# Attention into a tanh-shrink MLP: q and k fetched by squares of 32 and turned on VectorE from the fourth batch on, and the last store cut in two

## The chip, the cores and the metric

The kernel runs on one core of a Trainium2 chip. The metric is the time of one execution in microseconds, taken on the device. Its engines appear in the profile as PE (TensorE, with PEld for its weight loads), DVE (VectorE), ACT (ScalarE), POOL (GpSimd) and SP (SyncE, which here only issues transfers). Each takes its instructions in the order in which the program has them, and they wait for each other by semaphores.

## What is computed

Two blocks in a row. Attention: batch 8, 12 heads, 448 tokens, head width 64, with q and k normed by row before the product. Then an MLP of 3584 tokens, width 768, hidden width 2048:

```
rmsnorm(x, g) = x / sqrt(mean(x * x, axis=-1) + 1e-06) * g
scores = (1 / sqrt(64)) * rmsnorm(q, g_q) @ rmsnorm(k, g_k).T
attn   = exp(scores - max(scores)); attn = attn / (sum(attn) + 1e-09)
x      = (attn @ v), heads side by side: 3584 x 768
h = x @ w_in;  g = h - tanh(h);  out = g @ w_out
```

All data are float32 (the weights arrive as float64 and are rounded in the kernel).

## The kernel before

Work is cut into 48 **steps** (`steps`, L162): eight batches of six head pairs. A step s runs through several stages, and the stages of neighbouring steps are interleaved in a **slot**. There are three kinds: `first_slot` (L787) for the first batch, in which the weights are rounded; `early_slot` (L821) for the second; and `slot` (L849) for all others. The order inside a slot is written out by hand. In slot s the kernel finishes step s (sums of the exponentials, values, division), makes the scores of step s+1, turns q and k of step s+2, squares and norms those of step s+3 and loads those of step s+4. v of step s+2 is loaded here too.

Between these pieces `run(ns)` (L766) takes matmuls of the MLP from a generator, as many as fill the given time at 2.4 elements per ns. `gap_ns` (L778) spreads a batch's MLP evenly over its six slots: from the third batch on a `gap` is 14 matmuls, four gaps make a slot, and a matmul is two records in the trace. Whoever comes after a `run` in the program comes after its matmuls, and the instructions that empty their banks, in every engine's queue.

**q and k before.** `fetch` (L93) loads q with four neighbouring tokens on a partition (`"h (p c) d -> p h (c d)"`, 112 partitions, one transfer), k with three neighbouring keys on each of 128 partitions and 64 rest keys (four transfers). `squares_of` (L117) squares both on ScalarE. `norm_of` (L123) sums the squares on VectorE (L129), scales (L130), and takes the power -1/2 on GpSimd (L131), once for q and once for k. q is scaled by VectorE (`norm_q`, L400); k is not, its factor being the `scale` operand of the exponential (L444). `turn` (L406) makes both head-width-major: four TensorE transposes of k into one PSUM bank (L411), copied out by ScalarE with `g_col`, the product of g_q, g_k and 1/8 (L413), and four of q (L415), copied out at L419. `qT` and `kT` have two buffers each.

**Scores.** `scores` (L425) multiplies kT by qT (L438) for three chunks of 128 keys and a last one of 64, and ScalarE takes the exponential (L443). `add` and `add_last` (L451, L462) sum the chunks on VectorE (L459, L460, L467), so that `totals` (L495) needs fewer matmuls. There are five PSUM banks for attention (`sc`) and three for the MLP (`mm`), each set taken in turn (`bank_of`, L194).

**The MLP.** Both layers use Strassen-Winograd: seven products of half size per group in the order 1, 5, 6, 2, 3, 7, 4 (`ORDER`, L168; `products`, L557; the matmuls are L578). Products 2, 3 and 7 go on in the banks of 1, 5 and 6, and product 4 takes a new bank; hence the next use of a bank waits until VectorE or ScalarE has read the last. In the first layer (`hidden`, L599) VectorE makes the sums (L634 to L648), ScalarE the tanh (L614), VectorE or GpSimd the difference (L615), and both make factors of the second layer (L625 to L627, L659). Work that is not urgent is put on a list (`late["todo"]`) and issued at the end of the next product. Weights come from scratch memory into a ring of six slots (`ring_load`, L375): at the start of a product the load of the fifth product from there is issued (L382, L384), in SP's queue, together with all other loads and stores.

**The output.** `project` (L681) makes the second layer. `store` (L667) turns a 128 x 448 result on VectorE by blocks of 32 (L673), putting tokens back in natural order by reading them with a stride, since in q's loading a partition holds four neighbouring tokens, and issues four transfers from SP (L676), each of 32 x 14 runs of 128 bytes. The tanh buffer's two copies serve as its target.

Of the kernel before, what the change touches and what calls it, by code (L numbers as in the profile page):

```python
# [9 lines left out]
F32 = mybir.dt.float32  # L10
I32 = mybir.dt.int32
U32 = mybir.dt.uint32
AF = mybir.ActivationFunctionType
ALU = mybir.AluOpType
AX = mybir.AxisListType
# [5 lines left out]
NCH = 4  # L21
# [68 lines left out]
    nc.gpsimd.tensor_tensor(out=bits, in0=bits, in1=raw[:, :, 0], op=ALU.add)  # L90


def fetch(nc, name, t, pair):  # L93

    S = pair.shape[1]
    P = 128
    KF, KR = S // P, S % P
    if name == "q":
        nc.sync.dma_start(
            out=t.rearrange("p h c d -> p h (c d)"), in_=pair.rearrange("h (p c) d -> p h (c d)", c=NCH)  # L100
        )
        return
    full, rest = pair[:, : KF * P].rearrange("h (p c) d -> h p c d", c=KF), pair[:, KF * P :]
    if name == "v":
        last = t[:, :, KF]
        nc.sync.dma_start(
            out=t[:, :, :KF].rearrange("p h c d -> p h (c d)"), in_=full.rearrange("h p c d -> p h (c d)")
        )
    else:
        last = t[:, KF]  # L110
        for h in range(2):
            nc.sync.dma_start(out=t[:, :KF, h], in_=full[h])
    for r in range(2):
        nc.sync.dma_start(out=last[r * KR : (r + 1) * KR], in_=rest.rearrange("h p d -> p h d"))
# [19 lines left out]
def bounded_path(tc, ctx, q, k, v, moe_w_in, moe_w_out, out, g_col, ident, ones, half_ones, neg_half, early):  # L134
# [17 lines left out]
    nc = tc.nc  # L152
    B, H, S, D = q.shape
    DFF, DM = moe_w_out.shape
    P = 128
# [19 lines left out]
    def pool(name, **kw):  # L175
        return ctx.enter_context(tc.tile_pool(name=name, **kw))
# [27 lines left out]
    def load(s, names):  # L204
        b, hp = steps[s]
        for name in names:
            src = {"q": q, "k": k, "v": v}[name]
            if s == 0 and name != "v":
                t = early[name]
            else:  # L210
                shape = [CP, 2, NCH, D] if name == "q" else [P, NCH, 2, D] if name == "k" else [P, 2, NCH, D]
                t = nat.tile(shape, F32, name=f"{name}_nat", bufs=3 if name == "v" else 2)
                fetch(nc, name, t, src[b, 2 * hp : 2 * hp + 2])
            loaded[name, s] = t


# [189 lines left out]
    def turn(s, tk, tq):  # L406
# [12 lines left out]
        nc.scalar.copy(out=qT, in_=tq[:, :S])  # L419
        turned[s] = rr, kT, qT  # L420

    def sc_bank():
        return bank_of("sc")

    def scores(s, c):  # L425

        rr, kT, qT = turned[s]
        halves, keys, n = (1, P, S) if c < KF else (2, KR, HS)
        name, bufs = ("p", 2) if c < 2 else ("p_full", 1) if c < KF else ("p_last", 2)
        if c == 1:  # L430
            p = probs[s, 1] = probs[s, 0]
        else:
            p = probs[s, c] = pp.tile([P, 2, 2 if c < 2 else 1, n], F32, name=name, bufs=bufs)
        tiles = [sc_bank() for _ in range(2)]
        for i in range(halves):
            for h in range(2):
                r = slice(h * D, (h + 1) * D)
                nc.tensor.matmul(  # L438
                    tiles[h][i * keys : (i + 1) * keys, :n], lhsT=kT[r, c * P : c * P + keys],
                    rhs=qT[r, i * n : (i + 1) * n], start=True, stop=True,  # L440
                )
        for h in range(2):
            nc.scalar.activation(  # L443
                p[:, h, c if c < 2 else 0, :], tiles[h][:, :n], AF.Exp, scale=rr[:, 0, 2 * c + h : 2 * c + h + 1]  # L444
            )

    def full(s):
# [103 lines left out]
    def part(name):  # L551
        return tp.tile([P, 2, HS], F32, name=name)
# [111 lines left out]

        return products(b, 0, SETS, 2, HC, moving, done_with)

    def store(b, n, y):  # L667

        o = part("th").rearrange("p f s -> p (f s)")
        nc.vector.transpose(out=o, in_=y.rearrange("r (c p) -> r p c", c=NCH))  # L673
        for i in range(P // BL):
            d = n * P + i * BL
            nc.sync.dma_start(  # L676
                out=out[b * S : (b + 1) * S, d : d + BL].rearrange("(j t) d -> t j d", t=BL),
                in_=o[i * BL : (i + 1) * BL].rearrange("t (j d) -> t j d", d=BL),
            )

    def project(b):  # L681
        g, t = late["g"], late["t"]
        low, high = slice(0, HS), slice(HS, S)
        moving = {
            1: lambda f: g[:, f, low], 2: lambda f: g[:, f + HF, low], 3: lambda f: g[:, f + HF, high],
            4: lambda f: t[:, 2, f], 5: lambda f: t[:, 0, f], 6: lambda f: t[:, 1, f], 7: lambda f: g[:, f, high],
        }

        def done_with(j):
            y1, y2, s1 = (part(n).rearrange("p f s -> p (f s)") for n in ("s2", "s5", "s1"))  # L690

            def use(p, bank):
                v = bank[:, :HS]
                if p == 1:
                    nc.scalar.copy(out=s1[:, low], in_=v)
                elif p == 5:
                    nc.vector.tensor_tensor(out=y2[:, low], in0=v, in1=s1[:, low], op=ALU.add)
                elif p == 6:
                    nc.vector.tensor_tensor(out=y1[:, high], in0=v, in1=s1[:, low], op=ALU.add)
                elif p == 2:  # L700
                    nc.scalar.copy(out=y1[:, low], in_=v)
                elif p == 7:
                    nc.vector.tensor_tensor(out=y2[:, high], in0=v, in1=y2[:, low], op=ALU.add)
                    nc.vector.tensor_tensor(out=s1[:, low], in0=v, in1=s1[:, low], op=ALU.add)
                elif p == 3:
                    nc.vector.tensor_tensor(out=y1[:, high], in0=v, in1=y1[:, high], op=ALU.add)
                    late["todo"].append(lambda: store(b, j, y1))
                elif p == 4:
                    nc.vector.tensor_tensor(out=y2[:, low], in0=v, in1=s1[:, low], op=ALU.add)
                    late["todo"].append(lambda: store(b, HC + j, y2))  # L710

            return use

        return products(b, 1, HC, 1, HF, moving, done_with)

    def project_first(b):

        g = late["g"]
        for fn in late["todo"]:
            fn()  # L720
        late["todo"] = []
        took = 4 * S / ENGINE_NS
        for m in range(CD * CF):
            k, f = m // CF, m % CF
            n = (k + HC) % CD
            if f == 0:
                bank = mm_bank()
            if k < HC:
                weight(CF + HF + HF * (m + 1) // (HC * CF))
            elif m < HC * CF + 2:  # L730
                keep_w_out(PIECES - 2 + m - HC * CF)
            elif (m - HC * CF) % 4 == 0 and m - HC * CF <= 4 * HF:
                for fn in late["keep"]:
                    fn()
                late["keep"] = []
                combine_w_out((m - HC * CF) // 4 - 1)
            elif m == CD * CF - 12:
                ring_load(2)
                for fn in late["keep"]:
                    fn()  # L740
            elif m == CD * CF - 10:
                ring_load(4)
            nc.tensor.matmul(  # L743
                bank[:, :S], lhsT=w_out_row(f, n // HC)[:, n % HC * P : (n % HC + 1) * P], rhs=g[:, f, :],
                start=(f == 0), stop=(f == CF - 1),
            )
            if f == CF - 1:
                y = part("s2").rearrange("p f s -> p (f s)")
                nc.scalar.copy(out=y, in_=bank[:, :S])
                store(b, n, y)  # L750
            yield took
        wp_stack.close()
        late["tg"] = pool("tg", bufs=1)

    def mlp():
        late["todo"], late["keep"] = [], []
# [27 lines left out]
    def has(s):  # L784
        return 0 <= s < NS
# [63 lines left out]
    def slot(s):  # L849

        gap = gap_ns(s)
        if has(s + 1):
            scores(s + 1, KF)
        dn = sc_bank()
        av = [sc_bank() for _ in range(2)]
        last_values(s, av)
        totals(s, dn)
        divide(s, values(s, av))
        if has(s + 1):
            for c in range(KF):  # L860
                scores(s + 1, c)
        if has(s + 2):
            load(s + 2, "v")
        run(gap / 2)
        if has(s + 1):
            add(s + 1)
        run(gap / 2)
        if has(s + 2):
            turn(s + 2, sc_bank(), sc_bank())
        if has(s + 3):  # L870
            squares(s + 3)
        if has(s + 4):
            load(s + 4, "qk")
        for work, n, share in ((add_last, 1, 1), (norm, 3, 0.5), (norm_q, 3, 1)):
            run(gap * share)
            if has(s + n):
                work(s + n)
        run(gap / 2)

    load(0, "qk")  # L880
    load(1, "qk")
# [352 lines left out]
```

## Time and profile before

| | before |
|---|---|
| median of 11 runs | 1456.95 us (1455.11 to 1462.48) |
| the profiled execution | 1460.36 us |
| its span, first to last instruction | 1458.5 us |
| VectorE busy | 812.8 us (56%) |
| ScalarE busy | 453.0 us (31%) |
| GpSimd busy | 478.0 us (33%) |
| share of the 16 DMA engines, SP's queue | 59.5% |
| packets under 512 bytes | 164,725 of 267,894 |
| mean granted TensorE clock | 0.990 |

How to read the profile. A group's row gives line, engine, operation, what is written and read with shapes, the count, then busy time and mean ns of one, then the time for which the engine sat idle before it and what ended that. The **chain** is followed back from the last instruction, each time to what released it or to the instruction before it on its engine; what is not on it could be longer without moving the end. "issue" is time in which nothing shown was waited for. Durations are of one profiled execution; records of TensorE overlap, so the sum of their means is more than the time they take.

### The profile page before, as it was taken

How to read it: one execution, taken by the hardware profiler on the slowest of the kernel's cores; microseconds unless marked ns; L12 is line 12 of the kernel's file. 1: busy time of each engine (PE TensorE's matmuls, PEld its weight loads, DVE VectorE, ACT ScalarE, POOL GpSimd, SP SyncE). 2: the span in 40 equal slices, each digit the busy share in tenths (PEclk: the TensorE clock that was granted, in tenths of full speed). 3: DMA queues.
4: the chain of work that ended last, by engine and by line, in shares of the span. 5: the costliest groups of instructions: out<-in, count | busy, mean ns of one | idle time of the engine just before them, and what ended most of it. 6: DMA issues, size and time to landing. Idle time of an engine off the chain costs nothing.

```text
span 1458.5 us, 25920 instructions
## 1 busy us (share of the span) xinstructions
PE 1425.6 (98%) x10272; PEld 1202.1 (82%) x10272; DVE 812.8 (56%) x1246; ACT 453.0 (31%) x850; POOL 478.0 (33%) x378
## 2 busy tenths in 40 slices
PE   6999899999999999999999999999999999999997
PEld 3568654479988998899889989988998899899997
DVE  4999889766445564446644565446654456432312
ACT  6765553133212332223322233123322233211100
POOL 4656465223511243204421234212341134211310
PEclk9999899999999999999999999999999999999999
DMA  8769778854665555565536645654466555455663
GB/s 187 162 191 261 239 208 216 240 154 138 194 167 140 157 183 164 147 173 170 186 112 191 171 140 160 189 155 148 142 199 170 144 159 167 141 162 172 186 191 97
DMA packets 267894, 250.71 MB, mean 172 GB/s; under 512 B 164725, under 2 KB 210037, under 8 KB 267765
## 3 DMA queue, kind: packets, MB, share of 16 engines
q1 hardware_dynamic: 267760, 248.97, 59.5%
q8 instruction: 83, 1.36, 0.4%
q14 instruction: 47, 0.38, 0.1%
q10 hardware_dynamic: 4, 0.00, 0.0%
HBM read 215.48 MB, written 33.42 MB: 171 GB/s over the span
## 4 chain that ended last, share of the span: by engine, by line
PE 90%; DVE 5%; DMA 2%; SPq 2%; ACT 1%; issue 1%; POOL 0%; ACTq 0%
PE mm L578 64%; PE sc L438 9%; PE sc L489 6%; PE mm L743 4%; PE sc L477 1%; PE sc L510 1%; PE sc L411 1%; PE sc L415 1%; DVE w_out L82 1%; DVE rs L515 1%; DVE w_out L78 1%; DVE w_out L79 1%; DVE w_out L320 1%; DMA w_in<-w_out 0%; PE mm L489 0%
## 5 line engine op out<-in xcount | busy, mean ns | idle before, releaser
L131 POOL TENSOR_TENSOR rr<-rr,neg_half 112x8 f32<-112x8 f32 x96 | 156.5, 1649 | 370.6 <-DVE rr L130 370.5
L578 PE MATMUL mm<-xT,w_f 128*128 128x224 f32 x1392 | 276.6, 354 | 0.0
L578 PEld LDWEIGHTS mm<-xT,w_f 128*128 128x128 f32 x1392 | 261.3, 190 | 9.1 <-issue 9.1
L578 PE MATMUL mm<-gT,w_f 128*128 128x224 f32 x1344 | 263.0, 354 | 0.0
L578 PEld LDWEIGHTS mm<-gT,w_f 128*128 128x128 f32 x1344 | 252.8, 190 | 11.4 <-issue 11.1
L578 PE MATMUL mm<-tt,w_f 128*128 128x224 f32 x1044 | 209.6, 353 | 0.0
L615 POOL TENSOR_TENSOR gT<-s,th 128x448 f32<-128x448 f32 x96 | 117.9, 1236 | 260.9 <-ACT th L614 260.9
L578 PE MATMUL mm<-tg,w_f 128*128 128x224 f32 x1008 | 200.4, 353 | 0.0
L578 PEld LDWEIGHTS mm<-tt,w_f 128*128 128x128 f32 x1044 | 196.6, 190 | 3.9 <-issue 3.9
L578 PEld LDWEIGHTS mm<-tg,w_f 128*128 128x128 f32 x1008 | 189.5, 190 | 0.0
L438 PE MATMUL sc<-qT,kT 64*128 64x448 f32 (+1 forms) x960 | 169.9, 496 | 11.9 <-ACT p_last L443 8.9
L443 ACT ACTIVATE p<-sc,rr 128x448 f32<-128x448 f32 x192 | 106.0, 638 | 125.0 <-PE sc L438 125.0
L438 PEld LDWEIGHTS sc<-qT,kT 64*128 64x128 f32 (+1 forms) x960 | 73.4, 166 | 83.2 <-issue 48.8
L614 ACT ACTIVATE th<-s 128x448 f32<-128x448 f32 x96 | 55.5, 579 | 134.6 <-DVE s L640 56.6
L443 ACT ACTIVATE p_last<-sc,rr 128x224 f32<-128x224 f32 x96 | 37.8, 447 | 187.8 <-PE sc L438 187.7
L515 DVE RECIPROCAL rs<-sc 128x224 f32<-128x224 f32 x42 | 65.3, 1555 | 32.1 <-PE sc L510 32.0
L489 PE MATMUL sc<-p,v_nat 128*32 128x224 f32 x1344 | 79.1, 353 | 0.0
L538 POOL TENSOR_TENSOR tt<-xT,tt 128x224 f32<-128x224 f32 x23 | 17.1, 743 | 188.2 <-DVE xT L523 188.2
L743 PE MATMUL mm<-gT,w_out 128*128 128x448 f32 x192 | 76.9, 558 | 0.0
L523 DVE TENSOR_TENSOR xT<-sc,rs 64x224 f32<-64x224 f32 x168 | 65.2, 388 | 9.6 <-PE sc L489 2.2
L743 PEld LDWEIGHTS mm<-gT,w_out 128*128 128x128 f32 x192 | 36.9, 196 | 37.7 <-issue 36.7
L459 DVE TENSOR_TENSOR rows<-p 128x896 f32<-128x896 f32 x38 | 42.2, 1111 | 42.0 <-ACT p L443 42.0
(123 smaller groups left out, 1598.3 us busy)
## 6 DMA issues: line engine op xcount, KB each, us to landing
w_f<-w_in SPq DMA_DIRECT2D x196, 384.0 KB, 3.5
w_f<-w_out SPq DMA_DIRECT2D x147, 512.0 KB, 4.6
w_raw<-in_moe_w_out_dram SPq DMA_DIRECT2D x16, 768.0 KB, 5.1
out_dram<-th SPq DMA_DIRECT2D x192, 56.0 KB, 1.9
q_nat<-in_q_dram SPq DMA_DIRECT2D x47, 224.0 KB, 4.6
v_nat<-in_v_dram SPq DMA_DIRECT2D x48, 192.0 KB, 3.7
k_nat<-in_k_dram SPq DMA_DIRECT2D x94, 96.0 KB, 3.3
w_in<-w_out SPq DMA_DIRECT2D x21, 384.0 KB, 6.1
```

What stands on the lines that cost most here:

```text
L131: nc.gpsimd.tensor_tensor(out=r, in0=r, in1=neg_half[:rows], op=ALU.pow)
L438: nc.tensor.matmul(tiles[h][i * keys : (i + 1) * keys, :n], lhsT=kT[r, c * P : c * P + keys], rhs=qT[r, i * n : (i + 1) * n], start=True, ...
L443: nc.scalar.activation(p[:, h, c if c < 2 else 0, :], tiles[h][:, :n], AF.Exp, scale=rr[:, 0, 2 * c + h : 2 * c + h + 1])
L459: nc.vector.tensor_tensor(out=t, in0=p[0], in1=p[1], op=ALU.add)
L489: nc.tensor.matmul(av[n][r : r + BL, :HS], lhsT=v_nat[:, h, c, m * BL : (m + 1) * BL], rhs=p[c][:, h, n * HS : (n + 1) * HS], start=False, ...
L515: nc.vector.reciprocal(rs, dn[:, :HS])
L523: nc.vector.tensor_tensor(out=x[m * D : (m + 1) * D, n * HS : (n + 1) * HS], in0=av[n][m * D : (m + 1) * D, :HS], in1=rs[n * D : (n + 1) * ...
L538: eng.tensor_tensor(out=t2, in0=x22, in1=t1, op=ALU.subtract)
L578: nc.tensor.matmul(bank[:, f * HS : (f + 1) * HS], lhsT=w[:, c * width + f, :], rhs=moving[p](c), start=(first and f == 0 and c == 0), sto ...
L614: nc.scalar.activation(th, h, AF.Tanh, bias=0.0, scale=1.0)
L615: eng.tensor_tensor(out=g[:, rows, cols], in0=h, in1=th, op=ALU.subtract)
L743: nc.tensor.matmul(bank[:, :S], lhsT=w_out_row(f, n // HC)[:, n % HC * P : (n % HC + 1) * P], rhs=g[:, f, :], start=(f == 0), stop=(f == C ...
```

## The change

1. For batches 3 to 7 (`FIRST = 3`), q and k of a head pair go into one tile `[128, 2, 14, 32]`. A partition holds one token of each of 14 groups of 32, for one head and one half of the head width: eight transfers of 32 partitions x 14 runs of 32 floats.
2. Their squares are made in one ScalarE instruction. VectorE sums them; as each half of the width lies on other partitions, four copies between quarters of the partitions fetch the other half's sum, and an addition and a scaling follow. One power on GpSimd makes all factors, 28 columns. VectorE scales q and k in one instruction.
3. VectorE turns q and k by blocks of 32, straight from SBUF to SBUF. ScalarE multiplies kT by `g_col` in place. The eight TensorE transposes and their two PSUM banks are gone in these steps. As k is scaled, the exponential has the constant scale 1.0.
4. Tokens and keys are in natural order in these batches: v is fetched that way too (two transfers of 128 x 3 runs of 256 bytes in place of one of 768-byte runs; the rest as before), and the store's turn reads without a stride.
5. The slot's order: loading moves from step s+4 to s+3 and right behind v's load, the squares are made in the slot of s+2 after the sums of `add`, norming where the turns stood, then late sums, scaling, turn of q, turn of k, with half a gap between each and a whole gap at the end. The four gaps of a slot stay.
6. The very last result (last batch, last 128 columns) is stored in two halves of 224 tokens: the high half after product 7, the low one after product 4, with two of its four transfers from ScalarE's queue.

The diff, cut to its core:

```diff
+    def load_blocks(s):
+        b, hp = steps[s]
+        t = loaded["qk", s] = late["blocks"].tile([P, 2, NJ, BL], F32, name="qk_nat", bufs=2)
+        for i, src in enumerate((q, k)):
+            for h in range(2):
+                rows = src[b, 2 * hp + h].rearrange("(j t) (m d) -> m t j d", t=BL, d=BL)
+                for m in range(2):
+                    r = (2 * h + m) * BL
+                    nc.sync.dma_start(out=t[r : r + BL, i], in_=rows[m])
+
+    def square_blocks(s):
+        sq = normed[s] = late["blocks"].tile([P, 2, NJ, BL], F32, name="qk_n", bufs=1)
+        nc.scalar.activation(
+            sq.rearrange("p i j d -> p (i j d)"), loaded["qk", s].rearrange("p i j d -> p (i j d)"), AF.Square
+        )
+
+    def norm_blocks(s):
+        mine, other = (late["blocks"].tile([P, 2 * NJ], F32, name=name, bufs=2) for name in ("rr_mine", "rr_other"))
+        nc.vector.reduce_sum(mine, normed[s].rearrange("p i j d -> p (i j) d"), axis=AX.X)
+        for g in range(P // BL):
+            nc.vector.tensor_copy(out=other[g * BL : (g + 1) * BL], in_=mine[(g ^ 1) * BL : ((g ^ 1) + 1) * BL])
+        nc.vector.tensor_tensor(out=mine, in0=mine, in1=other, op=ALU.add)
+        nc.vector.tensor_scalar(out=mine, in0=mine, scalar1=1.0 / D, scalar2=1e-6, op0=ALU.mult, op1=ALU.add)
+        nc.gpsimd.tensor_tensor(
+            out=mine, in0=mine, in1=neg_half[:, :1].to_broadcast([P, 2 * NJ]), op=ALU.pow
+        )
+        normed["rr", s] = mine
+
+    def scale_blocks(s):
+        n, rr = normed[s], normed.pop(("rr", s))
+        nc.vector.tensor_tensor(
+            out=n.rearrange("p i j d -> p (i j) d"), in0=loaded.pop(("qk", s)).rearrange("p i j d -> p (i j) d"),
+            in1=rr[:, :, None].to_broadcast([P, 2 * NJ, BL]), op=ALU.mult,
+        )
+
+    def turn_blocks(s, i):
+        n = normed[s][:, i].rearrange("p j d -> p (j d)")
+        if i == 0:
+            qT = qkp.tile([P, S], F32, name="qT")
+            nc.vector.transpose(out=qT, in_=n)
+            turned[s] = qT
+            return
+        kT = qkp.tile([P, S], F32, name="kT")
+        nc.vector.transpose(out=kT, in_=n)
+        nc.scalar.mul(kT, kT, g_col)
...
-                p[:, h, c if c < 2 else 0, :], tiles[h][:, :n], AF.Exp, scale=rr[:, 0, 2 * c + h : 2 * c + h + 1]
+                p[:, h, c if c < 2 else 0, :], tiles[h][:, :n], AF.Exp,
+                scale=1.0 if rr is None else rr[:, 0, 2 * c + h : 2 * c + h + 1],
...
-        o = part("th").rearrange("p f s -> p (f s)")
-        nc.vector.transpose(out=o, in_=y.rearrange("r (c p) -> r p c", c=NCH))
+        o = part("th").rearrange("p f s -> p (f s)")[:, tokens]
+        y = y[:, tokens]
+        nc.vector.transpose(out=o, in_=y if b >= FIRST else y.rearrange("r (c p) -> r p c", c=NCH))
...
+            eng = nc.scalar if tokens.stop == HS and i % 2 else nc.sync
...
+                    if last:
+                        late["todo"].append(lambda: store(b, HC + j, y2, high))
...
+        if by_blocks(s + 3):
+            load_blocks(s + 3)
+        blocks = by_blocks(s + 2)
         run(gap / 2)
         if has(s + 1):
             add(s + 1)
+        if blocks:
+            square_blocks(s + 2)
         run(gap / 2)
-        if has(s + 2):
+        if blocks:
+            norm_blocks(s + 2)
+        elif has(s + 2):
             turn(s + 2, sc_bank(), sc_bank())
...
+        run(gap / 2)
+        if has(s + 1):
+            add_last(s + 1)
+        run(gap / 2)
+        if blocks:
+            scale_blocks(s + 2)
...
+        run(gap / 2)
+        if blocks:
+            turn_blocks(s + 2, 0)
+        run(gap / 2)
+        if blocks:
+            turn_blocks(s + 2, 1)
...
+        run(gap)
```

More of the change, by code (lines that the diff above doesn't have):

```diff
@@ L90, in round_weight_c, with fetch @@
     nc.gpsimd.tensor_tensor(out=bits, in0=bits, in1=raw[:, :, 0], op=ALU.add)
-def fetch(nc, name, t, pair):
+def fetch(nc, name, t, pair, in_order=False):
     S = pair.shape[1]
@@ L105, in fetch @@
         last = t[:, :, KF]
+    if in_order:
+        for h in range(2):
+            nc.sync.dma_start(out=t[:, h, :KF], in_=pair[h, : KF * P].rearrange("(c p) d -> p c d", p=P))
+    elif name == "v":
         nc.sync.dma_start(
@@ L212, in load @@
                 t = nat.tile(shape, F32, name=f"{name}_nat", bufs=3 if name == "v" else 2)
-                fetch(nc, name, t, src[b, 2 * hp : 2 * hp + 2])
+                fetch(nc, name, t, src[b, 2 * hp : 2 * hp + 2], by_blocks(s))
             loaded[name, s] = t
@@ L420, in turn, with by_blocks @@
         turned[s] = rr, kT, qT
+    FIRST, NJ = 3, S // BL
+    def by_blocks(s):
+        return has(s) and steps[s][0] >= FIRST
+    def load_blocks(s):
+        b, hp = steps[s]
+        t = loaded["qk", s] = late["blocks"].tile([P, 2, NJ, BL], F32, name="qk_nat", bufs=2)
+        for i, src in enumerate((q, k)):
+            for h in range(2):
+                rows = src[b, 2 * hp + h].rearrange("(j t) (m d) -> m t j d", t=BL, d=BL)
[34 more added lines that the diff above has]
+        nc.scalar.mul(kT, kT, g_col)
+        turned[s] = None, kT, turned[s]
+        del normed[s]
     def sc_bank():
@@ L665, in hidden, with store @@
         return products(b, 0, SETS, 2, HC, moving, done_with)
-    def store(b, n, y):
-        o = part("th").rearrange("p f s -> p (f s)")
-        nc.vector.transpose(out=o, in_=y.rearrange("r (c p) -> r p c", c=NCH))
+    def store(b, n, y, tokens=slice(0, S)):
+        o = part("th").rearrange("p f s -> p (f s)")[:, tokens]
+        y = y[:, tokens]
+        nc.vector.transpose(out=o, in_=y if b >= FIRST else y.rearrange("r (c p) -> r p c", c=NCH))
+        rows = slice(b * S + tokens.start, b * S + tokens.stop)
         for i in range(P // BL):
             d = n * P + i * BL
-            nc.sync.dma_start(
-                out=out[b * S : (b + 1) * S, d : d + BL].rearrange("(j t) d -> t j d", t=BL),
+            eng = nc.scalar if tokens.stop == HS and i % 2 else nc.sync
+            eng.dma_start(
+                out=out[rows, d : d + BL].rearrange("(j t) d -> t j d", t=BL),
                 in_=o[i * BL : (i + 1) * BL].rearrange("t (j d) -> t j d", d=BL),
@@ L690, in done_with @@
             y1, y2, s1 = (part(n).rearrange("p f s -> p (f s)") for n in ("s2", "s5", "s1"))
+            last = b == B - 1 and j == HC - 1
             def use(p, bank):
@@ L709, in use @@
                     nc.vector.tensor_tensor(out=y2[:, low], in0=v, in1=s1[:, low], op=ALU.add)
-                    late["todo"].append(lambda: store(b, HC + j, y2))
+                    late["todo"].append(lambda: store(b, HC + j, y2, *([low] if last else [])))
             return use
@@ L753, in project_first @@
         late["tg"] = pool("tg", bufs=1)
+        late["blocks"] = pool("blocks", bufs=1)
     def mlp():
@@ L866, in slot @@
             add(s + 1)
+        if blocks:
+            square_blocks(s + 2)
         run(gap / 2)
-        if has(s + 2):
+        if blocks:
+            norm_blocks(s + 2)
+        elif has(s + 2):
             turn(s + 2, sc_bank(), sc_bank())
-        if has(s + 3):
+        ahead = has(s + 3) and not by_blocks(s + 3)
+        if ahead:
             squares(s + 3)
-        if has(s + 4):
+        if has(s + 4) and not by_blocks(s + 4):
             load(s + 4, "qk")
[L874 to L877, printed above, removed]
         run(gap / 2)
+        if has(s + 1):
[3 more added lines that the diff above has]
+            scale_blocks(s + 2)
+        if ahead:
+            norm(s + 3)
+        run(gap / 2)
[4 more added lines that the diff above has]
+            turn_blocks(s + 2, 1)
+        if ahead:
+            norm_q(s + 3)
+        run(gap)
     load(0, "qk")
```

## The prediction

> **What bounds the kernel now.** I read the page from the top (busy time, slices), then the chain that ended last, then that chain in order of time in a stretch where the work repeats, then the groups by form for durations, and the last microseconds by timeline and by windows.
>
> ```profile
> PE 1425.6 (98%) x10272; PEld 1202.1 (82%) x10272; DVE 812.8 (56%) x1246; ACT 453.0 (31%) x850; POOL 478.0 (33%) x378
> ...
> PE   6999899999999999999999999999999999999997
> ...
> PEclk9999899999999999999999999999999999999999
> ```
>
> TensorE is busy in every slice after the first ones, at full clock. No other engine passes 56%. A busy PE could still be a slow PE, so the chain decides:
>
> ```profile
> 499.65 0.98 PE sc L438 x4
> 500.63 5.49 PE mm L578 x28
> 506.13 0.44 PE sc L411 x4
> 506.56 0.39 PE sc L415 x4
> 506.95 15.90 PE mm L578 x84
> 522.86 0.54 PE sc L438 x8
> ```
>
> This is one of the repeating slots (one head pair with its share of the MLP), 28.77 us long (500.63 to the same point at 529.41). Nothing but PE is on it, and each piece starts where the one before ended. Lines 411 and 415 are the turns of k and q: 0.44 + 0.39, that is 0.82 us per slot (506.13 to 506.95). MLP matmuls take 112 records in 21.2 us, two records to a matmul, so 0.19 us a record.
>
> **What the change removes from that path.** Of 48 head pairs, those of batches 3 to 7 are fetched by squares: 5 x 6 = 30. Each loses eight PE transposes. 30 x 0.82 = 24.6 us. Since PE never waits in these slots, all of it is on the path, as long as nothing else becomes late.
>
> Here a rule of the Trainium skill speaks against the edit: "VectorE: DVE Perf Modes", section "Rules for kernel authors", sends 128x128 transposes to TensorE when a PSUM destination will do and keeps VectorE for 32x32 blocks. By operation the rows partly agree: a VectorE turn of 128x448 takes 0.945 us against 0.44 for four PE turns. By the rule the edit would cost 2 x 0.945 - 0.82 = 1.1 us a slot. But the rule prices an operation alone; here PE is full and VectorE is not, so I count 0.82 off the path and put 1.9 us beside it.
>
> **What it adds beside the path, per slot.**
>
> ```profile
> L131 POOL TENSOR_TENSOR rr<-rr,neg_half 128x8 f32<-128x8 f32 x48 | 79.3, 1652 | 0.7 <-DVE rr L130 0.7
> ...
> L460 DVE TENSOR_TENSOR rows<-rows,p_full 128x896 f32<-128x896 f32 x38 | 47.9, 1260 | 4.3 <-DVE rows L459 0.5
> ...
> L673 DVE STREAM_TRANSPOSE th<-s 128x448 f32<-128x448 f32 x48 | 45.3, 945 | 13.0 <-ACT s L749 10.6
> ...
> L129 DVE TENSOR_REDUCE rr<-sq 128x8 f32<-128x512 f32 x48 | 32.5, 677 | 2.2 <-ACT sq L120 2.2
> ```
>
> VectorE loses two reductions (0.68 each), two small scalings (0.22 each) and the scaling of q (0.85 in these slots): 2.7 us. It gains a reduction of 896 (0.68 x 896/512 = 1.2), six small instructions at the 0.22 of the scalings (1.3; the four copies between quarters have no row of their own, so 0.1 to 0.3 each), a scaling of 896 (1.26, like L460) and two turns (1.9): 5.7 us. Net +3.0. From 568 to 740 us VectorE is busy 91.35 of 172 us, 15.3 per slot; 18.3 of a slot of 27.95 is 65%. There is room in sum.
>
> ScalarE loses two squares (1.27) and the copy of q (0.52), and gains one square of 896 (about 1.0). The exponentials lose their scale operand: COPY 128x448 takes 0.531, ACTIVATE with a column 0.632, so 0.1 each, 0.8 a slot. Whether PE gains by earlier exponentials is not shown: 12 records of scores take 2.69 us where 12 x 0.19 = 2.25 would do, and a part of these 0.4 us might go. Between 0 and 0.1 us a slot; I take 0, as PE shows no wait there on ScalarE.
>
> GpSimd loses two powers of 8 columns (1.65 each) and gains one of 28. Between a fixed price and one by column: 1.65 us, or with 0.19 fixed (224 columns of a plain operation take 0.66 us, 448 take 1.13) 0.19 + 28 x 0.18 = 5.3 us. I take 5.3: 8 columns cost more than 448 columns of an add, so a price by column is the nearer reading.
>
> **The wait that is added.** The scaling (scale_blocks) stands in VectorE's queue and waits for the power; behind it are the sums that empty the three mm banks, and TensorE waits for those. A product is 12 records, 2.27 us (16 records, 3.03 us, in the second layer). With three banks taken in turn a bank is wanted again two products after it was filled: the emptying has 4.5 us. I walk the tightest order I find, norming right behind the last product (4) of a group, with that product's end as zero. VectorE: sum 0.6, norming to 3.1, factors to 4.4, late sums (1.3) to 5.7, product 5's sum (filled at 4.5) to 6.3. The power runs 3.1 to 8.4, so VectorE stands 2.1 us; the scaling ends at 9.6. Product 6's sum (filled at 6.8) ends at 10.2: 3.4 of the 4.5. First turn to 11.2, product 2's (filled at 9.1) to 11.8: 2.7. Second turn to 12.8, then 0.63 on ScalarE, so kT is there at 13.4; its first user comes 14 matmuls (5.3 us) after the turn's place, which is behind product 2's use at 9.1, so after 14.4. Nothing stalls, with 1.0 us to spare. With a power of 1.65 us nothing is near. I count 0 and keep 0 to 0.5 us a slot, 0 to 15 in all; below zero is out, because the wait can't make PE faster. When cover is gone, each further us of power costs up to 1 us a slot.
>
> **The transfers.** q and k of a pair go from 5 transfers to 8 of 32x14 runs of 128 bytes, 3,584 runs in place of 1,248; v from 3 to 4 transfers with runs of 256 bytes. SP issues a transfer of that shape in 0.48 us (192 stores, median), so 3.8 + 2.5 us stand together in SP's queue ahead of the ring's weight loads. A ring load becomes free to go as its slot is released and is used five products later, 11.3 us. The 6.3 us of issue begin one product earlier than the next load could go, so it is held 4.0 us; with a landing of 3.5 to 4.6 us, 2.7 are left. What leaves in return is k's load standing in SP's queue for the turn (115 us of waiting in the span). The squares are used a slot after the issue. For the engines' time the last store is the row:
>
> ```profile
> 1453.00:1454.00 1.00, 0.00 (x0) 0.00 (x0) 0.00 (x0) 0.00 (x0) 0.00 (x0) 1.00 0.66 101
> 1454.00:1455.00 1.00, 0.00 (x0) 0.00 (x0) 0.00 (x0) 0.00 (x0) 0.00 (x0) 1.00 0.68 104
> 1455.00:1456.00 1.00, 0.00 (x0) 0.00 (x0) 0.00 (x0) 0.00 (x0) 0.00 (x0) 0.68 0.20 38
> ```
>
> The column before the last is the share of the 16 engines: 1.54 us x 16 = 24.6 for 4 x 448 = 1,792 runs, 13.7 ns each. 3,584 x 13.7 ns / 16 = 3.1 us a slot. The Trainium skill, "DMA: Bandwidth & Descriptors", section "Specifications", says that under 512 bytes the engines read, modify and write; taken as a doubling it would be 6.1 us. k's present runs of 256 bytes hold the engines about 1.35 us and q about 0.75, so the net is +1.0 by the row and +4.0 by the rule, on 16 of 28.8 us (share 0.56). Either leaves a quarter free. I count 0; with that cover gone, PE would wait at L578 for weights.
>
> **The last store.**
>
> ```profile
> 1450.72 0.39 DVE L709 TENSOR_TENSOR s<-mm,s 128x224 f32<-128x224 f32 x1 [2.34 <-PE mm L578]
> 1451.15 0.93 DVE L673 STREAM_TRANSPOSE th<-s 128x448 f32<-128x448 f32 x1
> ```
>
> Behind it come four SP issues of 0.5 us and the data, which end near 1455.3. Half the columns now go one product (3.0 us) earlier; the rest is a turn of 224 (0.3 to 0.45 less) and two issues on each of two queues (1.0 less), with half the data (up to 0.5 less). ScalarE's queue has no row for such an issue; at twice SP's price half of the gain would go. Between 0.6 and 1.9; I take 1.5. The turns of the other stores read their input in order now; they are off the path.
>
> **Sum.** The profiled execution took 1460.36 us, its span 1458.5. 1460.36 - 24.6 - 1.5 = 1434.3. The 11 runs have a median of 1456.95, 3.4 below; the same saving gives 1430.9. I say 1431.
>
> **Rivals.** (1) As worked out: 1431, between 1428 and 1435; 0.73. (2) The power is long and some slots stall 0.2 to 0.5 us: 6 to 15 us back, 1437 to 1446; 0.13. For it: 1.65 us for 8 columns, and 1.0 us of slack. Against: VectorE waited for the power just 3.6 us in 48 scalings. (3) Earlier exponentials and freer queues give PE some of the 0.4 us of the scores: 1424 to 1428; 0.06. (4) The removed time comes back as another wait of PE, for instance for weights behind 6.3 us of issue: within 3 us of 1457; 0.03. (5) Slower: the scaling waits so long for the power that the banks run dry in every slot. It decides from 0.87 us a slot on (26.1 / 30); at 1.5 us a slot it is 45 - 26 = +19, about 1476. That needs a power of some 8 us, or one of 5.3 queued behind 2.5 us of other GpSimd work in most slots; 0.05. That the turns stay on PE is excluded by the code.
>
> So faster 0.92, same 0.03, slower 0.05, where same is within 0.2% (2.9 us), about what a measurement of this kernel can tell. The range runs from 1427 to 1442: case 1, the near end of 3 and more than half of 2.
>
> **What would show it.** In the profile after: no L411 or L415 group behind the first 18 pairs; slots of 27.9 us with PE without idle time; the power's mean (1.7 or 5.3 us); VectorE's wait for it at the scaling, with nothing of it passed on to PE at the MLP's matmuls or at the scores; DMA share near 0.6; an end about 5.9 us behind the last sum (L709) in place of 7.4. Wrong would be PE idle at the MLP with VectorE as releaser (case 5 or 2), or with a weight load (case 4).

## The result and the profile after

| | before | after |
|---|---|---|
| median | 1457.41 us (31 runs) | 1429.35 us (8 runs, 1425.53 to 1431.78) |
| ratio after / before | | 0.9802, 95% interval 0.9788 to 0.9816 |
| profiled execution, its span | 1460.36, 1458.5 us | 1425.99, 1424.1 us |

The change saves 28.1 us by the medians; by the interval of the ratio it is 26.8 to 30.9. The page of the changed kernel, busy times and the slices of TensorE:

```profile
PE 1392.9 (98%) x10032; PEld 1172.5 (82%) x10032; DVE 867.1 (61%) x1397; ACT 412.2 (29%) x790; POOL 531.1 (37%) x348
...
PE   6999899999999999999999999999999999999998
```

TensorE is as full as it was; it simply has less to do. Work went to VectorE (+54 us) and GpSimd (+53 us), and left ScalarE (-41 us). One slot with squares, from the changed kernel's chain in order of time (start, length, what):

```profile
520.24 21.39 PE mm L640 x112
541.62 0.54 PE sc L499 x8
...
543.22 2.27 PE sc L551 x48
545.48 2.60 PE sc L499 x12
548.08 2.09 PE mm L640 x10
```

The MLP's 112 records run through without the turns in between, and the slot takes 27.84 us (520.24 to 548.08) where it was 28.77: 0.93 less. Turns and MLP together took 22.23 us before (500.63 to 522.86) and take 21.38 now, which is 0.84 of it; the other 0.09 lie in the last score piece, 2.60 where it was 2.69, as the chain of the kernel before has it:

```profile
526.72 2.69 PE sc L438 x12
```

All slots with squares but the first one have this length. The first still makes scores of the old kind and takes 27.93; the slot behind the last has no turns in either kernel and gains the 0.09. So it is 30 x 0.93 = 27.9 us. The end, from the start of the last 784 matmul records to the end of the span, is 155.2 us in place of 156.3. The two make 29.0.

The two profiled executions differ by more, 34.4 us of span. 5.5 us of it lie before the third batch's first slot (its matmuls begin at 299.23 before and at 293.77 after), where the change does nothing. Most of it is TensorE itself: up to there it is busy 274.1 us before and 269.3 after, with the same 2,097 matmul records, at a mean granted clock of 0.95 and 0.98. From 436 to 1268 us it is 1.00 in both. A single profile would have overstated the gain.

What was added, in groups by form of the changed kernel (busy time, mean ns | idle before, releaser):

```profile
L457 POOL TENSOR_TENSOR rr_mine<-rr_mine,neg_half 128x28 f32<-128x28 f32 x30 | 145.0, 4835 | 256.0 <-DVE rr_mine L456 256.0
...
L464 DVE TENSOR_TENSOR qk_n<-qk_nat,rr_mine 128x896 f32<-128x896 f32 x30 | 46.4, 1546 | 39.2 <-POOL rr_mine L457 37.5 <-DMA w_f<-w_out 1.6
...
L452 DVE TENSOR_REDUCE rr_mine<-qk_n 128x28 f32<-128x896 f32 x30 | 32.0, 1065 | 0.0
...
L474 DVE STREAM_TRANSPOSE qT<-qk_n 128x448 f32<-128x448 f32 x30 | 19.1, 638 | 0.5
```

The power of 28 columns takes 4.8 us, and VectorE waits for it at the scaling in 28 of 30 pairs, 37.5 us in all, up to 2.4 at once. TensorE's own list of waits in this stretch is empty: nothing of it is passed on.

### The profile page after: what moved, and what is told of

Its sections match the earlier page's. It is cut to its first block, busy times and chain, and to the rows that moved or that the text cites. A ratio compares the mean times of both kernels' runs of the same rounds, so it can differ in the third digit from the quotient of the medians.

```text
span 1424.1 us, 25690 instructions
## 1 busy us (share of the span) xinstructions
PE 1392.9 (98%) x10032; PEld 1172.5 (82%) x10032; DVE 867.1 (61%) x1397; ACT 412.2 (29%) x790; POOL 531.1 (37%) x348
## 4 chain that ended last, share of the span: by engine, by line
PE 92%; DVE 3%; DMA 2%; SPq 2%; ACT 1%; issue 1%; POOL 0%; ACTq 0%; DVEq 0%
PE mm L640 67%; PE sc L499 9%; PE sc L551 6%; PE mm L811 4%; PE sc L572 2%; PE sc L539 2%; DMA gT<-in_moe_w_in_dram 1%; DMA w_raw<-in_moe_w_out_dram 1%; PE mm L551 1%; SPq L118 1%; DVE rs L577 1%; SPq L265 0%; PE mm L572 0%; DVE w_out L82 0%; PE sc L419 0%
## 5 line engine op out<-in xcount | busy, mean ns | idle before, releaser
L457 POOL TENSOR_TENSOR rr_mine<-rr_mine,neg_half 128x28 f32<-128x28 f32 x30 | 145.0, 4835 | 256.0 <-DVE rr_mine L456 256.0
L677 POOL TENSOR_TENSOR gT<-s,th 128x448 f32<-128x448 f32 x96 | 122.6, 1283 | 200.6 <-ACT th L676 197.8
L504 ACT ACTIVATE p<-sc 128x448 f32<-128x448 f32 x120 | 55.5, 550 | 109.1 <-PE sc L499 109.1
L135 POOL TENSOR_TENSOR rr<-rr,neg_half 112x8 f32<-112x8 f32 (+1 forms) x36 | 59.5, 1676 | 57.1 <-DVE rr L134 56.6
L464 DVE TENSOR_TENSOR qk_n<-qk_nat,rr_mine 128x896 f32<-128x896 f32 x30 | 46.4, 1546 | 39.2 <-POOL rr_mine L457 37.5
```

Of the source, the lines that this page charges most:

```text
L135: nc.gpsimd.tensor_tensor(out=r, in0=r, in1=neg_half[:rows], op=ALU.pow)
L457: nc.gpsimd.tensor_tensor(out=mine, in0=mine, in1=neg_half[:, :1].to_broadcast([P, 2 * NJ]), op=ALU.pow)
L464: nc.vector.tensor_tensor(out=n.rearrange("p i j d -> p (i j) d"), in0=loaded.pop(("qk", s)).rearrange("p i j d -> p (i j) d"), in1=rr[:, ...
L504: nc.scalar.activation(p[:, h, c if c < 2 else 0, :], tiles[h][:, :n], AF.Exp, scale=1.0 if rr is None else rr[:, 0, 2 * c + h : 2 * c + h ...
L677: eng.tensor_tensor(out=g[:, rows, cols], in0=h, in1=th, op=ALU.subtract)
```

## The experiments

The theory: TensorE bounds every slot, so the gain is the time of its eight transposes, plus 0.09 us of the scores and 1.1 us of the end; all that was added hides, and the power is what comes nearest to not hiding. Rivals are named with each run. Ratios are to the kernel before, run on the same chip.

**E1: the last store whole again.**

```diff
-            last = b == B - 1 and j == HC - 1
+            last = False
```

> The changed kernel with its last result stored whole again. Theory (the end is set by the sum, the turn, the issues and the data behind the last product): the part from the start of the last 784 matmul records to the end of the span goes from 155.2 back to 156.3 us, the slots stay at 27.84 us, and the whole is 1.1 us longer (0.6 to 1.9), near 1430.5. Rival (the split store is hidden or costs as much as it saves, because ScalarE's queue issues slowly): no change.

1429.85 us, ratio 0.9811 (0.9791 to 0.9831). The time alone can't tell 0.5 us from nothing. The chain can: the last matmuls begin at 1271.54 of a span of 1428.1, so the end is 156.6 us, 1.3 more than in the changed kernel. The slots are unchanged. The split saves about 1.3 us here and 1.1 against the kernel before: the rival is out as far as one trace each can say it. In the changed kernel the last turn of 224 columns is followed by two issues on each of two queues; before, four stood on SP's alone:

```profile
1417.84 0.41 DVE L736 STREAM_TRANSPOSE th<-s 128x224 f32<-128x224 f32 x1
1418.27 1.51 SPq L741 DMA_DIRECT2D out_dram<-th  x2
1418.28 1.50 ACTq L741 DMA_DIRECT2D out_dram<-th  x2
```

```profile
1452.11 2.04 SPq L676 DMA_DIRECT2D out_dram<-th  x4
```

The second queue was to save 1.0 us and saves 0.5 here, which is where a part of the forecast 1.5 went. ScalarE is not the slower one: by single records its two issues take 0.39 and 1.07 us, SP's two beside them 0.32 and 1.15. In E1 the four on SP's queue take 2.9 us, so one trace of them says little more.

**E2: a column as the exponential's scale.**

```diff
-                scale=1.0 if rr is None else rr[:, 0, 2 * c + h : 2 * c + h + 1],
+                scale=ones[:, :1] if rr is None else rr[:, 0, 2 * c + h : 2 * c + h + 1],
```

> The changed kernel with a column of ones as the scale of the exponential in place of the constant 1.0. Theory A (the shorter exponential frees a PSUM bank earlier, so TensorE's 12 score records take 2.60 us in place of 2.69): the exponential of 448 columns goes from 0.55 to 0.64 us, the score piece back to 2.69, a slot from 27.84 to 27.93, 30 x 0.09 = 2.7 us in all, near 1432. Rival B (the score piece became shorter because of the other banks or the order of the loads): the exponential gets longer and the slot stays at 27.84, 1429.

1428.94 us, ratio 0.9815 (0.9791 to 0.9839): the expected 2.7 us are not resolved by the time. The slot shows them. Its exponential and its chain:

```profile
L504 ACT ACTIVATE p<-sc,ones 128x448 f32<-128x448 f32 x120 | 66.2, 634 | 103.8 <-PE sc L499 103.8
```

```profile
462.05 2.69 PE sc L499 x12
464.73 21.38 PE mm L640 x112
...
489.98 2.69 PE sc L499 x12
492.67 7.39 PE mm L640 x38
```

634 ns where the constant gives 550, the score piece is back at 2.69, the slot at 27.94 (464.73 to 492.67). So A: the second head's third chunk takes the bank of the very first exponential, and TensorE feels its length, though the list of waits names none. Single records say the same: in both kernels that chunk's first record starts 0.05 us after that exponential ends (519.22 and 519.17, with the column 491.65 and 491.60).

**E3: TensorE's turns back, for nobody.**

```diff
+    def idle_turns(s, tk, tq):
+        n = loaded["qk", s].rearrange("p i j d -> p (i j d)")
+        for c in range(NCH):
+            nc.tensor.transpose(tk[:, c * P : (c + 1) * P], n[:, c * P : (c + 1) * P], ident)
+        for c in range(NCH):
+            nc.tensor.transpose(tq[:, c * CP : (c + 1) * CP], n[:CP, c * P : (c + 1) * P], ident[:CP, :CP])
...
         if blocks:
+            idle_turns(s + 2, sc_bank(), sc_bank())
             norm_blocks(s + 2)
```

> The changed kernel with eight TensorE transposes per pair put back in their old place, into two PSUM banks that nobody reads; everything else, the turns on VectorE too, stays. Theory (the gain is the time of these transposes on TensorE, which waits for nothing): a slot goes from 27.84 to 28.66 us, 30 x 0.82 = 24.6 us back, near 1454. Rival (the gain came from the waits around the turns, for instance of SP's queue for k's turn or of ScalarE for the copies): less than half of it comes back, under 1441.

1455.81 us (12 runs), ratio 0.9978 (0.9964 to 0.9992): 26.5 us back. From its chain:

```profile
444.62 5.49 PE mm L647 x28
450.11 0.44 PE sc L452 x4
450.55 0.39 PE sc L454 x4
450.93 15.90 PE mm L647 x84
466.84 0.54 PE sc L506 x8
...
473.30 5.49 PE mm L647 x28
```

The same two pieces in the same place as before the change, and a slot of 28.68 (444.62 to 473.30): +0.84, times 30 is 25.2 us. No engine waits for these transposes, and still nearly all of the gain is gone. It was the time on TensorE, not the waits around the turns.

**E4: one matmul between the chunks of scores.** 12 records of scores take 2.60 us, where 12 of the MLP's take 2.27.

```diff
             for c in range(KF):
+                if c == KF - 1:
+                    run(4 * HS / ENGINE_NS)
                 scores(s + 1, c)
...
-        run(gap)
+        run(gap - (4 * HS / ENGINE_NS if has(s + 1) else 0.0))
```

> The changed kernel with one MLP matmul moved from the slot's last gap to a place between the second and the third chunk of scores. Theory A (the third chunk's second bank waits for the first exponential, so that 12 records take 2.60 us where 12 x 0.187 = 2.25 would do): the moved matmul runs in that wait, a slot goes from 27.84 to some 27.55 us, 36 slots x 0.3 = 9 to 11 us, near 1419. Rival B (the rest is a fixed cost of changing between matmuls of 64 and of 128 rows): the slot stays or grows by 0.1 to 0.4 us, since there are two more such changes, 1429 to 1440.

1444.87 us, ratio 0.991 (0.9891 to 0.9928): slower than the changed kernel by 15.5 us. A fell. A slot of the chain:

```profile
411.60 1.71 PE sc L499 x8
413.30 0.58 PE mm L640 x2
413.88 0.95 PE sc L499 x4
414.83 21.01 PE mm L640 x110
```

Eight records take 1.71 and four 0.95, together 0.06 more than twelve did, and the matmul in between 0.58 where it takes 0.38 in its row: the slot grows by 0.26 to 28.10. The wait that E2 found is gone here, since the first exponential ends (525.53) well before the third chunk starts (526.22). In the changed kernel it cost 0.14 us, so two more changes between matmuls of 64 and of 128 rows cost about 0.4, some 0.2 each (an estimate from single records of one slot; whether the rows do it or the change of operands is not told apart). That is B for some 9 us. The rest is another matter: one slot of six takes 29.42 to 29.46. Its chain:

```profile
537.07 5.11 POOL rr_mine L457
...
542.20 2.01 DVE qk_n L464
544.21 0.55 DVE s L698
544.75 0.04 issue
544.80 4.81 PE mm L640 x24
```

Here it is, the wait that the prediction feared: the power, the scaling that stands in VectorE's queue for it, the sum behind that (L698), and then TensorE. TensorE stands 1.1 us in five such slots (its list of waits: L698, 5.4 us, five times). Moving the order by one matmul was enough.

**E5: the power twice.**

```diff
+        nc.gpsimd.tensor_tensor(
+            out=spare, in0=mine, in1=neg_half[:, :1].to_broadcast([P, 2 * NJ]), op=ALU.pow
+        )
         nc.gpsimd.tensor_tensor(
             out=mine, in0=mine, in1=neg_half[:, :1].to_broadcast([P, 2 * NJ]), op=ALU.pow
         )
```

> The changed kernel with the power taken twice on GpSimd, the first time into a tile that nobody reads, so that the factors come 4.8 us later. Theory (the scaling stands in VectorE's queue until then; behind it are the sums that empty the three mm banks; a bank is wanted two products after it was filled, 4.5 us in the first layer and 6.1 in the second; the tightest sum of the changed kernel ends 3.3 us behind its product): the slots of the first layer stall, the tightest by up to 3.5 us, those of the second layer by little. TensorE's waits show VectorE's sums as releaser, and the whole takes 15 to 50 us more, 1444 to 1479. Rival (the queue has enough slack that VectorE's waiting never reaches TensorE): slots of 27.84, within 3 us of 1429.

1510.13 us, ratio 1.0346 (1.0328 to 1.0364): 80.8 us more than the changed kernel, and slower than the kernel before. Three slots of each batch, those of the first layer, take 31.2 to 35.6 us, the other three stay at 27.84; the sum is 78 us. The mechanism is the expected one, its size is past the expected range. The chain in the third of three such slots:

```profile
543.12 5.09 POOL rr_spare L458
...
548.29 4.80 POOL rr_mine L461
...
553.11 2.01 DVE qk_n L468
555.12 0.55 DVE s L702
...
555.71 7.49 PE mm L644 x24
```

L702 is the sum of product 6 (L698 in the changed kernel), behind the scaling. TensorE has stood 4.4 us for it. Its whole list of waits in these slots (total, times, longest):

```profile
PE mm L644 <- DVE s L702: 22.0, 5, 4.4
PE mm L644 <- DVE s L710: 15.6, 5, 3.4
PE mm L644 <- ACT s L698: 9.1, 5, 1.8
PE mm L644 <- DVE s L700: 6.9, 5, 1.4
```

That is 53.6 of the 78 us, and no wait is longer than the 4.8 us that were added. Most of the rest is a slower TensorE: the 24 records behind the wait take 7.49 us, where E4's 24 at the same place take 4.81. Two slots of one kind show what differs. In both TensorE stands 3.04 us; these are the pieces behind it in the chain, and the busy times with granted clock (third number from the end) of 3 us in each:

```profile
489.14 7.25 PE mm L644 x28
...
672.32 5.56 PE mm L644 x28
```

```profile
489.20:492.20 3.00, 3.00 (x9) 2.75 (x10) 2.90 (x6) 1.34 (x3) 1.68 (x2) 0.55 0.00 0
```

```profile
672.40:675.40 3.00, 3.00 (x16) 3.00 (x17) 2.90 (x6) 1.34 (x3) 1.70 (x2) 1.00 0.00 0
```

The first slot lost 5.0 us and the second 3.3. The granted clock fell to 0.50, for 3.4 to 6.8 us, at nine of the ten waits of 3.0 us and more; it stayed at 1.00 at the waits of 1.4 to 1.8 us, and at E4's of 1.1. Why the tenth was spared the traces don't show. Two things were thus missing from the forecast: this clock, and the tightest sum, which is 4.1 and not 3.3 us behind its product (see below). Lateness is not carried from slot to slot: the first power starts 8.7 us behind the slot's first MLP record here (543.12 and 534.44) and in the same slot of the changed kernel (528.90 and 520.24).

**E6: no power.** The power line is taken out, so q and k are scaled by the mean square and the result's values are others.

> The changed kernel without the power in the last 30 pairs (q and k are scaled by the mean square itself, so the power of -1/2 is left out). Theory (VectorE's 37.5 us of waiting for it are hidden): VectorE no longer waits for GpSimd at the scaling, the slots stay at 27.84 us, within 3 us of 1429. Rival (a part of the wait is on the path where no wait of TensorE is recorded): slots shorter by up to 1.2 us, 1393 to 1425.

1429.29 us, ratio 0.9797 (0.978 to 0.9815), slots of 27.84. 37.5 us of VectorE's waiting are gone, and nothing changes: they were hidden in full.

**E7: the loads twice.**

```diff
+                    nc.sync.dma_start(out=spare[r : r + BL, i], in_=rows[m])
                     nc.sync.dma_start(out=t[r : r + BL, i], in_=rows[m])
```

> The changed kernel with each of the eight transfers of a pair's squares issued twice, the first time into a spare tile: 3.8 us more of issue in SP's queue ahead of the weight loads and 3,584 more runs of 128 bytes a slot. Theory (a ring load may be 6 to 7 us late before TensorE waits for it, and was 4.0 late by the estimate): the queue now stands 10.1 us, which is past that slack by up to 1 us in first-layer slots, while DMA has room (share 0.63 to about 0.74); 0 to 1 us in 15 slots, 1429 to 1444. Rival A (SP has far more slack): exactly 27.84 us a slot, 1429. Rival B (the engines' bandwidth is near its end): every slot stalls by a us or more with weight loads as releaser, over 1459.

1428.69 us, ratio 0.9792 (0.9774 to 0.9811). All slots but one are at 27.84; one takes 28.24, with 0.2 us of TensorE waiting for a ring load. So neither SP's queue nor the engines are near their end: rival A but for that slot, and the estimated slack was too small. From 436 to 1268 us, changed kernel and this one (busy times by engine, clock, DMA share, GB/s):

```profile
436.00:1268.00 832.00, 832.00 (x6092) 731.14 (x6092) 507.43 (x856) 205.25 (x425) 307.73 (x189) 1.00 0.63 166
```

```profile
436.00:1268.00 832.00, 831.84 (x6085) 730.25 (x6078) 504.81 (x859) 206.31 (x426) 305.93 (x189) 1.00 0.71 181
```

The share goes from 0.63 to 0.71 for 3,584 runs a slot: 0.08 x 27.84 x 16 / 3,584 = 10 ns a run, within what two digits of a share give.

**E8: two pairs more.** The squares begin with the fifth pair of the third batch; its first four pairs keep TensorE's turns, with q fetched in natural order, and the batch's stores read without a stride.

```diff
-    FIRST, NJ = 3, S // BL
+    FIRST, NJ = 2, S // BL
...
-        return has(s) and steps[s][0] >= FIRST
+        return has(s) and s >= FIRST * NP + 4
...
+        if in_order:
+            for h in range(2):
+                nc.sync.dma_start(out=t[:, h], in_=pair[h].rearrange("(c p) d -> p c d", c=NCH))
+            return
```

> The changed kernel with the squares also for the last two pairs of the third batch, whose other four pairs keep TensorE's turns but fetch q in natural order. Theory (0.93 us per pair that is moved, wherever it lies): two more slots at 27.84 in place of 28.77, 1.9 us less, near 1427.5; q's fetch by runs of 256 bytes is hidden. Rival (the first slots with squares pay for a transition): the two slots stay above 28 us, 1429 or more.

1427.36 us, ratio 0.9772 (0.9753 to 0.9791). In the chain the slots fall to 27.85 two slots earlier, so the 1.9 us are there; by time the interval overlaps the changed kernel's, and a better version is likely but not measured.

## Why the prediction was right

- **The path.** 0.82 us a slot, 24.6 in all. Before and after differ there by 0.84, and E3, which puts the same instructions back, finds 0.84 a slot (25.2 us) and 26.5 us by the medians. Right.
- **Earlier exponentials.** The prediction had 0 to 0.1 us a slot and took 0, because TensorE shows no wait on ScalarE. It is 0.09, 2.7 us in all (E2). This is the term that was set too low, and nearly all that parts 1431 from 1429.
- **The power.** The reading by column gave 5.3 us; it is 4.8 in most slots and 5.1 in the tightest. The fixed reading, 1.65, was wrong.
- **The wait at the scaling.** The walk said that VectorE stands about 2 us and that nothing reaches TensorE, with 1 us to spare. In the changed kernel it stands at most 2.4 us. The order that was walked occurs in the third first-layer slot of each batch. From its timeline (start, length, what, idle before and releaser):

```profile
694.90 4.70 PE L640 MATMUL mm<-tt,w_f 128*128 128x224 f32 x24
...
695.95 5.09 POOL L457 TENSOR_TENSOR rr_mine<-rr_mine,neg_half 128x28 f32<-128x28 f32 x1 [1.67 <-DVE rr_mine L456]
...
699.44 6.97 PE L640 MATMUL mm<-xT,w_f 128*128 128x224 f32 x36
701.00 1.13 POOL L677 TENSOR_TENSOR gT<-s,th 128x448 f32<-128x448 f32 x1
701.07 2.02 DVE L464 TENSOR_TENSOR qk_n<-qk_nat,rr_mine 128x896 f32<-128x896 f32 x1 [2.11 <-POOL rr_mine L457]
...
703.01 0.61 DVE L698 TENSOR_TENSOR s<-mm,s 128x448 f32<-128x448 f32 x1
```

  Product 6 is the second half of the 24 records and ends at 699.4. Its sum (L698) ends near 703.55, 4.1 us behind, and product 7 wants the bank at 4.5. The walk had 3.4 there. From the norming on its times come out to 0.2 us but for one term: the scaling was put at 1.26 us, and it takes 2.0 here, while GpSimd works beside it. In the first slots of a batch, with GpSimd idle, it takes 1.09 (477.14). So nothing reached TensorE, as forecast, but with 0.4 us to spare and not 1.1, and that is partly luck. E6 shows that the wait is hidden, E5's 4.4 us of waiting for 4.8 of power that the slack is 0.4. That each further us costs up to 1 us a slot was right for the wait; a slot lost up to 7.7, because the clock fell as well.
- **VectorE's sum.** Forecast +3.0 us a slot. From 436 to 1268 us VectorE was busy 440.4 us before and 507.4 after, by slots 15.2 and 17.0: +1.8. The scaling took more (1.55 in the mean against 1.26) and the turns less (0.64 against 0.945).
- **The transfers.** Forecast +1.0 us of the engines a slot by the row and +4.0 by a doubling. The share went from 0.55 to 0.63, 15.8 to 17.5 us a slot: +1.7. No doubling is seen: E7 gives 10 ns a run, and by the trace's records of single packets one of 128 bytes holds its engine 13 ns (median), one of 256 bytes 18, one of 512 bytes 27. SP's queue has more room than the 2.7 us of the estimate.
- **The last store.** Forecast 1.5 (0.6 to 1.9), found 1.1 to 1.3, as the second queue saved 0.5 of the 1.0 us counted for it (E1).

Rival 5 is the one worth keeping: its mechanism exists, and the changed kernel sits about 0.4 us from where it begins. A lengthening between nothing and 4.8 us was not tried; the point is read from the trace, and E5's waits agree with it.

## What to carry to other kernels

When one engine is on the chain in every piece, an instruction taken from it is worth its whole time, even if another engine then needs longer for it (here two turns of 0.64 us for 0.82). What decides is not the other engine's load in percent but the longest time that a queue stands in front of something the full engine waits for: walk the tightest slot by hand, with bank or buffer deadlines, before adding an in-order wait, and price an instruction by what runs beside it there. Past the slack the loss can be more than the wait, as E5's clock shows. And count a slot in the trace: a tenth of a microsecond in each of thirty is clear there when the medians can't show it.

## What the hardware showed that was not expected

- A VectorE turn of 128x448 float32 takes 0.94 us when it reads with a stride of 448 bytes and 0.64 us when it reads in order; a half of 224 in order takes 0.41.
- GpSimd's power is paid by column: 1.65 us for 8, 4.8 for 28, so about 0.16 us a column and 0.4 fixed.
- A change of TensorE between 64-row score matmuls and 128-row matmuls costs about 0.2 us (estimate from E4).
- After waits of 3.0 us and more the granted TensorE clock was 0.50 for 3.4 to 6.8 us, in nine cases of ten (E5); after waits of 1.8 us and less it was 1.00.
- The same VectorE product of 128x896 takes 1.09 us while GpSimd is idle and 2.0 while GpSimd works beside it. That GpSimd is the cause is not shown; no run takes its work away there.
- Two stores issued on each of two queues took 1.5 us side by side, four on one queue 2.0 and 2.9 (one trace each).
